# A planned attention, Fourier and MLP kernel: where the zero products begin, which engine fills buffers, how many rows are buffered, and what the planner is told of loads

## The chip, the cores and the metric

The kernel runs on one core of a Trainium2 chip. The metric is the time of one execution in device microseconds (us), the median of several runs. The profile shows one execution: TensorE (PE, with its weight loads as PEld), VectorE (DVE), ScalarE (ACT), GpSimd (POOL), the sync engine (SP) and the DMA engines.

## What is computed

Four batches of 8 heads, 768 positions and 64 elements per head. Attention is local: each chunk of 32 positions looks at 8 memory keys and a window of up to 56 keys around it. The result, laid out as 768 x 512 per batch, goes through a two-dimensional Fourier transform of which the real part is kept, and through an MLP with a residual:

```python
scores = scale * np.matmul(q_c, k_full.transpose(0, 1, 3, 2))   # per chunk of 32
a = softmax(scores); x[chunk] = np.matmul(a, v_full)
mixed = np.real(fft(fft(x, axis=1), axis=2))
u = x + mixed
un = (u - mean(u)) / sqrt(var(u) + 1e-6)
out = u + np.maximum(un @ w_ch1, 0.0) @ w_ch2                   # 512 -> 2048 -> 512
```

## The kernel before

**Work units.** Attention goes over 16 pairs of heads, n = 0 to 15, four per batch. A pair is loaded by GpSimd (`e_load_qk`, L283: q and k, cast to bf16 on the way; three buffers each) and by the sync queue (`e_load_v`, L292 to L301: v and the memory values in many short rows; four buffers `va`). TensorE turns q and k (`turn`, L310), ScalarE copies the turned q out (L319), VectorE the turned k for batch 0 and ScalarE for the rest (L337). Then come, in two halves g, the scores (`e_scores`, L348), the exponential (`e_exp`, L356, ScalarE), the product with the values (`e_values`, L369) and the normalisation (`e_norm`, L379 and L380, VectorE), which writes into `xs[b]`. The PSUM tiles `sc` and `xa` exist once each, so scores of one half wait until the exponential of the half before has read them.

**Fourier and MLP.** When a batch's `xs` is whole, the row transform runs as products with cosine and sine tables (L531 for batch 0, L437 for the others), then the column transform (L542), whose result VectorE adds into `xs` (L548). VectorE takes mean and variance (L554), ScalarE writes the centred row tile `un` in fp16 (`e_un`, L560), six tiles per batch. For batch 0 TensorE turns `un` (L567) and VectorE copies it into `unT`; for the later batches a transposing DMA on the sync queue does it (`e_flip`, L572), and the `un` buffer is free again when that DMA has landed. The MLP is `e_ch1` (`ph`, L593), ReLU on ScalarE (`hT`, L600), `e_ch2` (`pc`, L607), the residual on VectorE (L613) and the store. Its weights, eight GpSimd loads of 512 KB as written, are issued between the loads of batch 1.

**Order.** The order of all instructions on each engine is fixed when the kernel is built. Each piece of work is a task with an engine, a cost in us, a rank, the tasks it comes after, and the buffers that it takes and gives. `Plan.order` plays this through: whenever an engine is free, it gives it the task of lowest rank that is ready by the planned times. On the chip an engine then runs its instructions strictly in that order, each waiting for what it needs. The plan's numbers therefore move no instruction's duration, only its place. `LAG` is what passes between the end of a task and its use elsewhere; a load is done a lag after its bytes (`moved`, in us of wire time) have gone through its queue, plus `late` for batches after the first. TensorE's costs count double before `WARM`. The first transform and earlier pairs have lower ranks than later pairs; MLP products rank last and fill what is left.

**Zero products.** [...]So the planner puts small products with a zero matrix (`e_fill`, L650) wherever TensorE would be idle, from the moment the task `filling[0]` is placed until `filling[1]` is:

```python
if e == "PE" and self.filling and self.filling[0]["at"] is not None \
        and self.filling[1]["at"] is None:
    cost = self.FILL * (2.0 if now < self.WARM else 1.0)
```

`filling[0]` is the first zero product itself (`t_fill`, rank -1), `filling[1]` follows the first low half of batch 0's row transform.

**Fills at the start.** VectorE zeroes the last rows of the three k buffers (L634, one task) ahead of the identity cast (L628), which every turn needs; it zeroes the edges of the four v buffers (L255 to L257), computes the angles of the tables (S, then D: L668 to L676), casts and spreads the memory keys (L729, L738, L332) and copies the first k (L337). ScalarE zeroes the 32 low rows of the four v buffers (`e_low_rows`, L271): two early, two after the sines. GpSimd sets single entries of the edges to one (`e_edge_ones`). A small copy on GpSimd, the gate (L701), waits for the v of the fourth pair; q and k loads of batch 1 and the weights stand behind it.

Of the kernel before, what the change touches and what calls it, by code (L numbers as in the profile page):

```python
# [21 lines left out]
MEM0 = 32  # L22
# [14 lines left out]
class Plan:  # L37
# [1 line left out]

    LAG = {"PE": 0.2, "DMA": 1.4}
    FIRST = 45.0
    WARM = 7.0
    SLACK = 0.7
    FILL = 0.17
    filling, fill = None, None
# [14 lines left out]
    def order(self):  # L62
        now, idle, wire = 0.0, {}, {}
        waiting = {}
        for t in self.tasks:
            waiting.setdefault(t["engine"], []).append(t)
        for ts_ in waiting.values():
            ts_.sort(key=lambda t: (t["rank"], t["no"]))
        gives = []
        placed = []  # L70
        while any(waiting.values()):
            for tag in [g for g in gives if g[0] <= now]:
                gives.remove(tag)
                self.free[tag[1]] += 1
            moved = False
            for e, ts_ in waiting.items():
                if idle.get(e, 0.0) > now:
                    continue
                held = False
                for t in ts_:  # L80
                    slack = (self.SLACK if e == "PE" and now > self.FIRST and not t["filler"]
                             else 0.0)
                    if held and not t["loose"]:
                        continue
                    if any(a["done"] is None
                           or (a["end"] > now if a["engine"] == e else a["done"] > now - slack)
                           for a in t["after"]):
                        held = held or (e == "SP" and not t["loose"])
                        continue
                    if t["behind"] is not None and t["behind"]["at"] is None:  # L90
                        continue
                    need = {}
                    for tag in t["take"]:
                        need[tag] = need.get(tag, 0) + 1
                    if any(self.free[tag] < m for tag, m in need.items()):
                        held = held or (e == "SP" and not t["loose"])
                        continue
                    for tag in t["take"]:
                        self.free[tag] -= 1
                    cost = t["cost"] * (2.0 if e == "PE" and now < self.WARM else 1.0)  # L100
                    idle[e] = t["end"] = now + cost
                    if t["moved"]:
                        wire[e] = max(wire.get(e, 0.0), now + cost) + t["moved"]
                        t["done"] = t["end"] = wire[e] + self.LAG["DMA"] + t["late"]
                        if t["push"] and wire.get("SP", 0.0) > now:
                            wire["SP"] += t["moved"]
                            for o in placed:
                                if o["engine"] == "SP" and o["done"] > now:
                                    o["done"] += t["moved"]
                                    o["end"] = o["done"]  # L110
                    else:
                        t["done"] = now + cost + self.LAG.get(e, 0.07)
                    for tag in t["give"]:
                        gives.append((t["done"], tag))
                    t["at"] = now
                    placed.append(t)
                    ts_.remove(t)
                    moved = True
                    break
                else:  # L120
# [3 lines that stand above are left out]
                        idle[e] = now + cost  # L124
                        placed.append(dict(engine="PE", cost=cost, emit=self.fill, at=now,
                                           done=now + cost))
                        moved = True
            if not moved:
                times = ([v for v in idle.values() if v > now] + [g[0] for g in gives]
                         + [t["done"] + x for t in placed for x in (0.0, self.SLACK)  # L130
                            if t["done"] + x > now])
                assert times, [(t["engine"], t["no"], t["take"]) for ts_ in waiting.values()
                               for t in ts_[:2]]
                now = min(x for x in times if x > now)
        self.end = max(t["done"] for t in placed)
        return placed
# [3 lines left out]
def kernel(  # L140
# [49 lines left out]
    seq = [(b, pr) for b in range(B) for pr in (0, 2, 1, 3)]  # L190

    plan = Plan(dict(qs=NS, ks=NS, va=NV, kTb=NKT, qT=2, tr=1, sc=1, xa=1, e1=3,
                     xsb=3, fold=2, hl=1, up=4, dn=4, acc=2, mlp=2, un=3, unT=2, hT=1, osb=3))
    add = plan.add
    MLPS = 1000000

# [71 lines left out]

    def e_low_rows(i):
        low = va[i][0:MEM0].rearrange("p h t c -> p (h t c)")  # L270
        nc.scalar.copy(low, zero[0:MEM0].to_broadcast([MEM0, 2 * NT * 66]))  # L271

    def e_mkf():
        for par in range(2):
# [280 lines left out]
        nc.vector.bn_aggr(mu_of[b][:, kt, :], st6)  # L555

    def e_un(b, kt):
        un_of[b, kt] = un = fpool.tile([P, DM], FP16, tag="un", bufs=3, name="un")

        nc.scalar.activation(un, xs[b][:, kt, :], AFT.Identity, bias=mu_of[b][:, kt, 0:1],  # L560
                             scale=-1.0)
# [65 lines left out]
    def e_idb():  # L627
# [3 lines left out]
        nc.vector.tensor_copy(turn_b[:, KOFF + QP:KP], ident[0:KP, KOFF + QP:KP])  # L631

    t_idb = add("DVE", 0.5, e_idb, [t_id], rank=-16.5)
    t_kz = add("DVE", 0.8, lambda: [nc.vector.memset(ks[i][QP:KP], 0.0) for i in range(NS)],  # L634
               rank=-16.95)
    t_low, LOW = {}, 110
    for i in range(NV):
        e_ = add("DVE", 0.4, lambda i=i: e_edges(i), rank=-20 if i == 0 else -17.4 + 0.1 * i)
        t_ones[i] = add("POOL", 0.7, lambda i=i: e_edge_ones(i), [e_], rank=-3.5 if i == 0 else 2)
        t_low[i] = add("ACT", 1.45, lambda i=i: e_low_rows(i), [t_zero, e_],  # L640
                       rank=(0, 1, LOW, LOW + 1)[i])
    t_masks = add("POOL", 0.6, e_masks, rank=16)
    dz = cpool.tile([P, P], BF16)
# [33 lines left out]
            y, r, -1.0, r, ALU.mult, ALU.max), t3, rank=ANG[nm] + 3)  # L677


    kept, t_mk, t_lv, t_ck, t_after = {}, {}, {}, {}, {}  # L680
    t_norm = {}

    def last(key, n, back):
# [4 lines left out]
    def attention(n):  # L688
# [1 line left out]
        b, pr = seq[n]  # L690
        first = b == 0
        lq, lk = [add("POOL", 0.9, lambda i=i: e_load_qk(n, i), take=(("qs", "ks")[i],),
                      moved=1.3, late=0.0 if b == 0 else 2.0, behind=t_gate if n == HP else t_ck.get(n - 1),
                      rank={0: -4 + i, 1: -1.2 + 0.1 * i}.get(n)) for i in range(2)]
        lv = add("SP", 2.5, lambda: e_load_v(n), [t_ones[n] if n < NV else None],
                 take=("va",), moved=4.0, late=0.0 if b == 0 else 2.0)
        t_lv[n] = lv
        t_ck[n] = lk
        if n == HP - 1:
# [6 lines left out]
        eq = add("ACT", 0.80, lambda: e_qT(n), [tq], take=("qT",), give=("tr",),  # L706
                 rank=SINES - 0.5 if n == 0 else None)
        ktag = "acc" if first else "tr"
        tk = add("PE", 0.43, lambda: e_turn_k(n), [lk, t_idb, t_kz], take=(ktag,), give=("ks",))
        mk = t_mk[n] = add("DVE", 0.2, lambda: e_mkT(n), [t_mkT, t_kTz[n % NKT], t_mk.get(n - 1)],  # L710
                           take=("kTb",))
        ek = add(dve[0], 1.25 if dve[1] else 1.04, lambda: e_kT(n, dve[1]), [tk, mk], give=(ktag,))
        for g in range(2):
            s_ = add("PE", 0.32, lambda g=g: e_scores(n, g), [eq, ek], take=("sc",),
                     give=("qT", "kTb") if g == 1 else ())
            x_ = add("ACT", 2.4 if (n, g) == (0, 0) else 1.12, lambda g=g: e_exp(n, g),
                     [s_, t_masks, t_after.get(n)], take=("e1",), give=("sc",))
            tag = "xa"
            v_ = add("PE", 0.85, lambda g=g: e_values(n, g), [x_, lv, t_low[n % NV]], take=(tag,),
                     rank=len(plan.tasks) + (50 if (n, g) == (2, 1) else 25) if first else None,  # L720
                     give=("e1", "va") if g == 1 else ("e1",))
            take = ("xsb",) if g == 0 and n % HP == 0 else ()
            t_norm[n, g] = add("DVE", 0.78, lambda g=g: e_norm(n, g),
                               [v_, t_norm[n - n % HP, 0] if (n % HP, g) != (0, 0) else None],
                               take=take,
                               give=(tag,))
# [39 lines left out]
                    [t_angle["S"], t_angle["D"] if par == 2 else None, t_sin], rank=SINES)  # L766
    t_sines = t_sin
    for i in range(2, NV):
        t_low[i]["behind"] = t_sin
    t_neg = add("DVE", 0.6, e_negatives, [t_sines], rank=100)  # L770
    t_rows = add("DVE", 1.0, e_table_rows, [t_sines, t_neg], rank=101)
    t_idh = add("DVE", 0.25, lambda: nc.vector.tensor_copy(ident_h, ident), [t_id], rank=140)
# [15 lines left out]
    def first_fourier():  # L788
# [12 lines left out]
        for g in range(2):  # L801
            t_mid[g] = add("DVE", 0.4, lambda g=g: g_mid(g), [t_norm[2, g], t_norm[3, g]],
                           rank=len(plan.tasks) + 8)
            for par in range(2):
                for ab in range(2):
# [6 lines left out]
                    lo = add("DVE", 0.48, lambda par=par, ab=ab, g=g: g_lo(par, ab, g), [hi],  # L812
                             give=("fold",) if end else ())
                    if (par, ab, g) == (0, 0, 0):
                        plan.filling = (t_fill, add("PE", 0.0, lambda: None, [lo], give=("mlp",)))
                    tag = ("acc", "mlp")[par]
                    rw = add("PE", 2.0 if (par, ab) == (0, 1) else 1.0,
                             lambda par=par, ab=ab, g=g: g_rows(par, ab, g),
# [153 lines left out]
```

## Time and profile before

The median of three runs is 313.76 us (312.69 to 319.26); the profiled execution spans 314.6 us.

| engine | busy, us | share | instructions |
|---|---|---|---|
| PE | 298.4 | 95% | 3178 |
| PEld | 185.4 | 59% | 3178 |
| DVE | 170.4 | 54% | 371 |
| ACT | 164.8 | 52% | 293 |
| POOL | 37.5 | 12% | 76 |

| group | count | busy, us |
|---|---|---|
| first MLP product `ph` (L593) | 512 | 94.4 |
| second MLP product `pc` (L607) | 384 | 86.1 |
| values `xa` (L369) | 768 | 29.7 |
| zero products `idle` (L650) | 101 | 23.4 |
| low rows `va` on ScalarE (L271) | 4 | 5.9 |

A busy TensorE can be busy with zero products, so its share says nothing of useful work in the first slices. The chain that ended last follows the last instruction back to what released it, step by step; where it changes from PE to a DMA and back, TensorE had been waiting. In the timeline a line gives start, duration, engine, line, operation, result and operands; the bracket behind it tells how long the engine had been idle before it and what ended that. The list of DMA issues gives, for one load, the time from issue to landing.

### The profile page before, as it was taken

How to read it: one execution, taken by the hardware profiler on the slowest of the kernel's cores; microseconds unless marked ns; L12 is line 12 of the kernel's file. 1: busy time of each engine (PE TensorE's matmuls, PEld its weight loads, DVE VectorE, ACT ScalarE, POOL GpSimd, SP SyncE). 2: the span in 40 equal slices, each digit the busy share in tenths (PEclk: the TensorE clock that was granted, in tenths of full speed). 3: DMA queues.
4: the chain of work that ended last, by engine and by line, in shares of the span. 5: the costliest groups of instructions: out<-in, count | busy, mean ns of one | idle time of the engine just before them, and what ended most of it. 6: DMA issues, size and time to landing. Idle time of an engine off the chain costs nothing.

```text
span 314.6 us, 7551 instructions
## 1 busy us (share of the span) xinstructions
PE 298.4 (95%) x3178; PEld 185.4 (59%) x3178; DVE 170.4 (54%) x371; ACT 164.8 (52%) x293; POOL 37.5 (12%) x76
## 2 busy tenths in 40 slices
PE   5899999998999994999999999999999999999994
PEld 2457668876666773467577656675454454554641
DVE  7937896984398884079879488776100101002001
ACT  5657665687884372776477722753271360440710
POOL 7506322141020003000000100000200000000000
PEclk9589999999999998799999999999999999999999
DMA  6997999998991389941003301002500101101001
GB/s 113 191 167 134 209 205 197 197 198 167 180 150 44 101 134 132 134 95 42 33 35 53 52 24 44 33 2 50 150 2 33 68 2 43 57 2 67 33 35 67
DMA packets 60289, 28.93 MB, mean 92 GB/s; under 512 B 48480, under 2 KB 56672, under 8 KB 60256
## 3 DMA queue, kind: packets, MB, share of 16 engines
q1 hardware_dynamic: 47168, 11.61, 22.5%
q0 software_dynamic: 9344, 10.49, 21.1%
q10 hardware_dynamic: 3744, 6.36, 5.5%
q8 instruction: 25, 0.41, 0.6%
q14 instruction: 8, 0.07, 0.1%
HBM read 30.28 MB, written 6.29 MB: 116 GB/s over the span
## 4 chain that ended last, share of the span: by engine, by line
PE 86%; DMA 7%; SPq 2%; ACT 2%; DVE 1%; issue 1%; POOL 1%; ACTq 0%; POOLq 0%
PE pc L607 26%; PE ph L593 26%; PE xa L369 8%; PE pm L542 6%; PE idle L650 6%; PE ps L437 5%; PE ps L531 3%; PE sc L348 3%; DMA va<-in_mem_v_dram 2%; DMA qs<-in_q_dram 2%; PE trk L310 2%; PE trq L310 2%; DMA unT<-un 2%; SPq L292 2%; DVE osb L613 1%
## 5 line engine op out<-in xcount | busy, mean ns | idle before, releaser
L593 PE MATMUL ph<-unT,w_sb 128*128 128x384 f16 x512 | 94.4, 331 | 5.6 <-ACT hT L600 4.9
L600 ACT ACTIVATE hT<-ph 128x384 f16<-128x384 f32 x128 | 61.1, 492 | 66.3 <-PE ph L593 65.6
L607 PE MATMUL pc<-w_sb,hT 128*128 128x512 f16 x384 | 86.1, 380 | 0.0
L593 PEld LDWEIGHTS <-w_sb 128*128 128x128 f16 x512 | 48.6, 98 | 40.0 <-issue 11.1
L613 DVE SCALAR_TENSOR_TENSOR osb<-pc,rstd,xsb 128x512 f32<-128x512 f32 x24 | 18.0, 749 | 84.0 <-PE pc L607 84.0
L607 PEld LDWEIGHTS <-hT 128*128 128x128 f16 x384 | 36.6, 98 | 42.5 <-issue 0.3
L356 ACT ACTIVATE e<-sc,mbias 128x384 f32<-128x384 f32 x64 | 33.6, 580 | 10.7 <-PE sc L348 10.5
L369 PE MATMUL xa<-va,e 128*64 128x65 f32 x768 | 29.7, 226 | 0.8 <-DMA va<-in_mem_v_dram 0.8
L369 PEld LDWEIGHTS xa<-va,e 128*64 128x64 f32 x768 | 25.3, 138 | 7.6 <-issue 5.7
L560 ACT ACTIVATE un<-xsb,mu_s 128x512 f16<-128x512 f32 x24 | 17.1, 719 | 14.1 <-DMA unT<-un 7.8
L650 PE MATMUL idle<-dz 128*128 128x384 bf16 x101 | 23.4, 373 | 1.0 <-DVE zero L230 1.0
L449 ACT CAST up<-ps 128x386 f16<-128x386 f32 x16 | 9.7, 604 | 20.3 <-PE ps L437 14.7
L548 DVE TENSOR_TENSOR xsb<-pm,xsb 128x512 f32<-128x512 f32 x24 | 16.2, 675 | 5.7 <-PE pm L542 5.4
L380 DVE TENSOR_TENSOR xsb<-xa,zs 128x384 f32<-128x384 f32 x32 | 17.8, 557 | 1.1
L554 DVE BATCH_NORM_STATS2 st<-xsb 128x6 f32<-128x512 f32 x24 | 16.4, 682 | 0.5
L283 POOL DMA_DIRECT2D qs<-in_q_dram x16 | 10.5, 658 | 42.2 <-PE trq L310 37.0
L379 DVE RECIPROCAL zs<-xa 128x6 f32<-128x6 f32 x32 | 6.1, 189 | 17.1 <-PE xa L369 17.0
L283 POOL DMA_DIRECT2D ks<-in_k_dram x16 | 10.4, 648 | 39.1 <-PE trk L310 34.9
L319 ACT COPY qT<-trq 128x768 bf16<-128x768 bf16 x16 | 12.8, 799 | 3.7 <-PE trq L310 3.7
L650 PEld LDWEIGHTS <-dz 128*128 128x128 bf16 x101 | 9.5, 108 | 8.5 <-issue 3.0
L337 ACT COPY kTb<-trk 128x1056 bf16<-128x1056 bf16 x12 | 12.5, 1041 | 2.8 <-PE trk L310 2.8
L453 DVE TENSOR_TENSOR up<-ps,up 128x386 f16<-128x386 f32 x16 | 9.5, 597 | 8.0 <-ACT up L449 8.0
(124 smaller groups left out, 331.7 us busy)
## 6 DMA issues: line engine op xcount, KB each, us to landing
va<-in_v_dram SPq DMA_DIRECT2D x32, 220.0 KB
out_dram<-osb ACTq DMA_DIRECT2D x24, 256.0 KB
w_sb<-in_moe_w_ch_dram POOLq DMA_DIRECT2D x8, 512.0 KB, 17.0
qs<-in_q_dram POOLq DMA_DIRECT2D x16, 192.0 KB, 6.7
ks<-in_k_dram POOLq DMA_DIRECT2D x16, 192.0 KB, 6.6
va<-in_mem_v_dram SPq DMA_DIRECT2D x32, 24.0 KB
va<-in_v_dram SPq DMA_DIRECT2D x32, 22.0 KB
va<-in_v_dram SPq DMA_DIRECT2D x16, 32.0 KB
```

Source lines behind the costliest of these rows:

```text
L283: nc.gpsimd.dma_start(dst[n % NS][0:QP], src[b, 2 * pr:2 * pr + 2].rearrange("h (p j) d -> p h (j d)", j=RB))
L356: nc.scalar.activation(e1[:, :, :, ts(half, 32)], sc[:, :, 0:6, ts(half, 32)], AFT.Exp, bias=mbias[:, half:half + 1], scale=1.0 / math.sqr ...
L369: nc.tensor.matmul(xa[64 * half:64 * half + 64, st, hh, 0:65], e1[:, hh, t6, :], v1[:, hh, 6 * g + t6, 0:65], start=True, stop=True)
L380: nc.vector.tensor_tensor(xs[b][:, 3 * g:3 * g + 3, 2 * pr * D:(2 * pr + 2) * D] .rearrange("p s (h d) -> p s h d", h=2), xa[:, :, :, 0:D] ...
L542: nc.tensor.matmul(pm[:, par, :], lhs, rhs[:, par, :], start=(im == 0), stop=(im == 3))
L554: nc.vector.bn_stats(st6, xs[b][:, kt, :])
L560: nc.scalar.activation(un, xs[b][:, kt, :], AFT.Identity, bias=mu_of[b][:, kt, 0:1], scale=-1.0)
L593: nc.tensor.matmul(ph[:, 0:384], w1_sb[:, dt, ts(ht, P)], unT_of[b][:, dt, sh * 384:(sh + 1) * 384], start=(dt == 0), stop=(dt == NDT - 1))
L600: nc.scalar.activation(hT_of[b, sh][:, ht, :], ph_of.pop((b, sh, ht))[:, 0:384], AFT.Relu, bias=0.0, scale=-1.0)
L607: nc.tensor.matmul(pc_of[b, sh, stl], hT_of[b, sh][:, ht, ts(stl, P)], w2_sb[:, ht, :], start=(ht == 0), stop=(ht == NHT - 1))
L613: nc.vector.scalar_tensor_tensor(osb, pc_of.pop((b, sh, stl)), rstd_of[b][:, st:st + 1], xs[b][:, st, :], ALU.mult, ALU.add)
L650: nc.tensor.matmul(fill_of[0][:, 0:384], dz, strided(dz, 0, [[0, 3], [1, P]]), start=True, stop=True)
```

## The change

It has five parts. (1) Zero products begin when the first scores have been placed, not at the very start, and `WARM` goes from 7 to 14. (2) The planner's numbers for loads follow a trace: a GpSimd load counts as done 2.8 us after its bytes instead of 1.4, and the loads of the first four pairs have longer wire times of their own. (3) The zero rows of the first k buffer are a task of their own, ahead of the identity cast; those of the other two come after the S angles (rank -12), and the edges of v buffers 2 and 3 come among the D angles (rank -9.5, -9.4). (4) The low rows of v buffers 2 and 3 are filled by a GpSimd memset, placed behind the fourth k load, not by ScalarE. (5) `un` has six buffers instead of three. The purpose is to take waiting and filling work away from the engines that carry the start of the kernel, and to let ScalarE write all rows of a batch without waiting for a transposing DMA.

```diff
-    LAG = {"PE": 0.2, "DMA": 1.4}
+    LAG = {"PE": 0.2}
-    WARM = 7.0
+    WARM = 14.0
...
-                        t["done"] = t["end"] = wire[e] + self.LAG["DMA"] + t["late"]
+                        t["done"] = t["end"] = wire[e] + (2.8 if e == "POOL" else 1.4) + t["late"]
...
-                     xsb=3, fold=2, hl=1, up=4, dn=4, acc=2, mlp=2, un=3, unT=2, hT=1, osb=3))
+                     xsb=3, fold=2, hl=1, up=4, dn=4, acc=2, mlp=2, un=6, unT=2, hT=1, osb=3))
...
     def e_low_rows(i):
         low = va[i][0:MEM0].rearrange("p h t c -> p (h t c)")
-        nc.scalar.copy(low, zero[0:MEM0].to_broadcast([MEM0, 2 * NT * 66]))
+        if i < 2:
+            nc.scalar.copy(low, zero[0:MEM0].to_broadcast([MEM0, 2 * NT * 66]))
+        else:
+            nc.gpsimd.memset(low, 0.0)
...
-        un_of[b, kt] = un = fpool.tile([P, DM], FP16, tag="un", bufs=3, name="un")
+        un_of[b, kt] = un = fpool.tile([P, DM], FP16, tag="un", bufs=6, name="un")
...
-    t_kz = add("DVE", 0.8, lambda: [nc.vector.memset(ks[i][QP:KP], 0.0) for i in range(NS)],
-               rank=-16.95)
+    t_kz = add("DVE", 0.5, lambda: nc.vector.memset(ks[0][QP:KP], 0.0), rank=-16.95)
+    t_kzs = add("DVE", 1.0, lambda: [nc.vector.memset(ks[i][QP:KP], 0.0) for i in range(1, NS)],
+                rank=-12)
...
-        e_ = add("DVE", 0.4, lambda i=i: e_edges(i), rank=-20 if i == 0 else -17.4 + 0.1 * i)
+        e_ = add("DVE", 0.4, lambda i=i: e_edges(i), rank=(-20, -17.3, -9.5, -9.4)[i])
...
-        t_low[i] = add("ACT", 1.45, lambda i=i: e_low_rows(i), [t_zero, e_],
+        t_low[i] = add("ACT" if i < 2 else "POOL", 1.45, lambda i=i: e_low_rows(i), [t_zero, e_],
                        rank=(0, 1, LOW, LOW + 1)[i])
...
-                      moved=1.3, late=0.0 if b == 0 else 2.0, behind=t_gate if n == HP else t_ck.get(n - 1),
+                      moved=1.3 if b else (2.1, 2.1, 1.4, 1.4)[n], late=0.0 if b == 0 else 2.0,
+                      behind=t_gate if n == HP else t_ck.get(n - 1),
...
-                 take=("va",), moved=4.0, late=0.0 if b == 0 else 2.0)
+                 take=("va",), moved=4.0 if b else (4.4, 6.5, 4.9, 3.6)[n], late=0.0 if b == 0 else 2.0)
...
-        tk = add("PE", 0.43, lambda: e_turn_k(n), [lk, t_idb, t_kz], take=(ktag,), give=("ks",))
+        tk = add("PE", 0.43, lambda: e_turn_k(n), [lk, t_idb, t_kz if n == 0 else t_kzs], take=(ktag,), give=("ks",))
...
     for i in range(2, NV):
-        t_low[i]["behind"] = t_sin
+        t_low[i]["behind"] = t_ck[HP - 1]
...
-                        plan.filling = (t_fill, add("PE", 0.0, lambda: None, [lo], give=("mlp",)))
+                        plan.filling = (t_sc[0, 0], add("PE", 0.0, lambda: None, [lo], give=("mlp",)))
```

More of the change, by code (lines that the diff above doesn't have):

```diff
@@ L677 @@
             y, r, -1.0, r, ALU.mult, ALU.max), t3, rank=ANG[nm] + 3)
-    kept, t_mk, t_lv, t_ck, t_after = {}, {}, {}, {}, {}
+    kept, t_mk, t_lv, t_ck, t_after, t_sc = ({} for _ in range(6))
     t_norm = {}
@@ L715, in attention @@
                      give=("qT", "kTb") if g == 1 else ())
+            t_sc[n, g] = s_
             x_ = add("ACT", 2.4 if (n, g) == (0, 0) else 1.12, lambda g=g: e_exp(n, g),
```

## The prediction

> **What bounds the kernel now.** I read the page's slices first, then the chain of work that ended last in order of time, then the timeline around each break in it, then the times from issue to landing of single loads. Slices (40 of 7.9 us):
>
> ```profile
> PE   5899999998999994999999999999999999999994
> PEclk9589999999999998799999999999999999999999
> DMA  6997999998991389941003301002500101101001
> ```
>
> TensorE looks full from the second slice on, and the DMA engines from the second to the ninth. But in the windows, line L650, the product with zeros, fills 23.3 of the first 44.2 us. The chain shows where it stands in the way:
>
> ```profile
> 13.57 0.81 PE trk L310 x16
> 14.38 4.68 PE idle L650 x19
> 19.06 0.28 PE sc L348 x12
> ...
> 118.73 6.00 DMA unT<-un
> 124.83 0.72 ACT un L560
> 125.56 0.39 ACT hT L600
> 125.98 4.74 PE ph L593 x16
> ```
>
> Nineteen zero products lie between the last K turn and the first scores, although VectorE's copy of K, which the scores need, ends at 13.65 + 1.25 = 14.90 (first line below; the two after it are the row fills on ScalarE between exponentials):
>
> ```profile
> 13.65 1.25 DVE L337 COPY kTb<-trk 128x1056 bf16<-128x1056 bf16 x1
> 21.67 1.49 ACT L271 COPY va<-zero 32x1584 f32<-32x1584 f32 x1
> 26.54 1.50 ACT L271 COPY va<-zero 32x1584 f32<-32x1584 f32 x1
> ```
>
> Second break, 118 to 126 us: ScalarE stands at `un` until a transposing DMA has given a buffer back; behind it in its order stands the `hT` that TensorE needs:
>
> ```profile
> 124.83 0.72 ACT L560 ACTIVATE un<-xsb,mu_s 128x512 f16<-128x512 f32 x1 [5.33 <-DMA unT<-un]
> 125.98 6.12 PE L593 MATMUL ph<-unT,w_sb 128*128 128x384 f16 x24 [4.59 <-ACT hT L600]
> ```
>
> Third, what the loads allow. The GpSimd queue is backed up: q of the eighth pair, issued at 44.84, took 19.0 us (lands 63.8); its k, issued at 47.55, lands at 66.6, as TensorE comes to turn it. Soon after, values wait for a v load:
>
> ```profile
> ks<-in_k_dram POOLq DMA_DIRECT2D x1, 192.0 KB, 19.1
> ```
>
> TensorE's side of it:
>
> ```profile
> 66.65 0.55 PE L310 MATMUL trk<-turn_b,ks 100*64 100x100 bf16 x16 [0.18 <-DMA ks<-in_k_dram]
> 72.90 0.80 PE L369 MATMUL xa<-va,e 128*64 128x65 f32 x20 [0.83 <-DMA va<-in_mem_v_dram]
> ```
>
> So there are three regimes: a start-up chain to 44 us, a DMA-fed stretch to about 73, and TensorE alone after that (68.34 busy of 68.5 us from 126.5 to 195; 108.18 of 108.6 from 202 to 310.6).
>
> **What the Trainium skill says.** "TensorE: Matmul & The Clock Gate", section "What's actually happening": the array drops to half rate after an idle window of about 3.4 us and comes back after about as long busy, the window running freely. The trace agrees roughly: 2.64 us idle before 7.60 brought 0.85 us Q turns (0.53 later); from 14.31 full rate was back at 17.17, in 2.9 us; after the 4.59 us gap the clock was 0.50 in the window 125.98 to 129.80. "DMA: Bandwidth & Descriptors", section "Queues, rings and completion order": each DMA engine takes turns between queues, packet by packet; that agrees with GpSimd loads of one size taking 3.7 us (issued 26.39) when the sync queue had just run dry and 19 us later. "SBUF — State Buffer", section "Who interferes with whom": GpSimd collides with VectorE only over the shared ports, and a GpSimd instruction that only writes isn't held up by VectorE's two-input ones; no run here shows a fill this long.
>
> **Part by part.**
>
> *Zero products from the first scores on.* Gone are the fillers before the scores: all but one of the 15 at the very start (3.91 us in which TensorE has nothing to do) and the 24 of 7.6 to 19. The first scores move from 19.00 to just after the K copy. That copy ends a nearly gapless run of VectorE work, and the same work stays ahead of it in rank: ks zeros (1.57), edge fills of buffers 2 and 3 (1.3 together), the D angles (2.4); the change reorders them. So 14.90 stays and the scores start near 15.05: **-3.95**. TensorE is then cold. Scores and fillers run at half rate for about 2.9 us, to 18.0. Between first and second scores the trace has 13 fillers and two turns (3.36 us warm); the plan's 2.67 us (exponential 2.4 and lags) leaves room for about 9 beside the turns, 2.6 us warm; with 1.2 of it done by 18.0, the second scores stand at 19.4 against 22.64: **-3.2**. Bounds: -4.6 (ScalarE alone: 15.65 + 1.28 table + 1.05, then scores at 18.1) and -2.4 (all 13 fillers).
>
> *Row fills of buffers 2 and 3 to GpSimd.* 2 x 1.5 us leave ScalarE between exponentials. In the planner's costs each pushes the next exponential back about 0.85 us (1.45 less the 0.6 that ScalarE would have waited for scores): **-1.6** by the last scores of batch 0, so about **-4.8** in all there (35.71 to 30.9). On GpSimd a fill costs between 1.4 and 3.5 us: its memset of 128x384 bf16 took 424 ns, so 1584 elements 1.75 us by count and 3.5 by bytes. I take 1.75. It is placed behind the fourth k load, where GpSimd idles 13.7 us before the gate, and values need the rows only after 26 us: nothing on the path.
>
> *Zeros and edges later.* The identity cast waited for ks zeros until 7.32; without two edge fills and two zero fills ahead (1.3 + 1.05) the first Q turn waits only for its load, 6.45 instead of 7.60. The first K turn waits for its load (9.60) anyway: nothing. GpSimd's edge ones for buffer 2 now wait on an edge fill that ends near 10.6; the loads of the fourth pair queue behind them, some 1 us later. Landing then at 19.3 and 21.0, they may cost the last turns of batch 0 about 0.5 us, inside the next term.
>
> *Planned costs and lags.* They cost no instruction; they move things in the written order. Even the new costs make the planned landing of the eighth pair far earlier than the traced 63.8 and 66.6 (lag +1.4 us, gate about +3.4), so the planner still doesn't see that backlog, and I expect the same TensorE order around it.
>
> *What of -4.8 survives the loads.* The rows of the first transform, 44.3 before, could start at 39.5, and TensorE would be at the eighth Q turn at 59.7 instead of 64.48. Its load lands at 63.8. It can move only with the gate (the fourth v load, landed 25.88) and with the DMA time that lies idle: shares of 18 to 26 us and the hole at 24 to 26.3 (share 0.63), which the fifth v load can now use as its buffer comes free sooner. An upper bound is some 3.5 us, a lower one 0: the v queue runs ahead sooner and takes its turns from the q/k queue. A stall of 3 to 4 us also brings the half clock, 1.5 us or so. The 0.83 us wait for v is likely to go. I take **-1.0**, between +1 and -4.8.
>
> *Six `un` buffers.* All six rows of a batch have a buffer; no activation waits for its own batch's transposes. The 4.59 us gap goes, and with it the slow clock after it: 16 matmuls took 4.74 us, 16 at the later 1.41 per 8 take 2.82, so 1.92. Sum **-6.5**. TensorE is the bound from there to the end, so it stays. The other `un` waits (0.42, 2.06 us on ScalarE) have no gap in TensorE beside them: nothing. Bounds: -7 and, if the transposes' order on the sync queue brings a wait elsewhere, -1.
>
> Sum: 313.76 - 6.5 - 1.0 = **306.3**.
>
> **Rivals.** *A, the loads don't hold it*: the gate comes early, or MLP products are planned into the wait. Then 313.76 - 6.5 - 4.8 = 302.5. For it: the DMA's idle time at 18 to 26, and w1 landed by 47. Against: the products' inputs are turned behind the eighth Q turn in TensorE's order. *B, the wait moves*: a new in-order hole takes what six buffers give, and only the front's 1.0 is left: 312.8. For it: every order is rewritten; against: the gap has one cause, and ScalarE no other DMA to wait for. *C, slower*: stalls at the eighth pair plus cold clock (+2), a new gap like that at 121 (+6.5), the old one half gone (-3): 319.3. For it: shifting fixed orders made such gaps before; against: it needs several at once.
>
> **From these to the numbers.** Mine 0.52, A 0.20, B 0.20, C 0.08. Two per cent is 307.5. About four fifths of mine lies below it (0.42) and all of A: faster 0.62. The rest of mine, B and a quarter of C: same 0.32. Slower 0.06. The range runs from a little below A, 301.0, to nearly B, 312.0.
>
> **What would show it.** Right: first scores near 15 us with zero products only after them; no L271 on ScalarE after 7 us; no `un` waiting for a DMA, and full clock at 118 to 126, moved; a wait on q or k of the eighth pair near 60 to 66 that eats the front's gain. Wrong: the eighth k landing before 64 (A), a TensorE gap over 3 us after 100 (B or C), or first scores after 17.

## The result, and the profile after

The changed kernel takes **308.87 us** (median of four executions, 308.59 to 309.45). The kernel before, run beside it, took 312.69 to 319.93 us, median 316.51. The ratio of the two is **0.985** (95% interval 0.981 to 0.989): faster, but not by the 2% on which the forecast had put its largest chance. The ratio leaves out executions more than 1.5% above a kernel's fastest, and since 38 of 59 further executions of the kernel before (311.26 to 319.81 us) are of that kind, medians of all executions are given beside the ratios below.

The changed kernel's slices of the span (40 of 7.7 us; busy tenths of TensorE, its granted clock, busy tenths of the DMA engines):

```profile
PE   1399999999999999999989999999999999999994
...
PEclk9999999999999999999999999999999999999999
DMA  6989999999944925821361011004201101001011
```

Against the slices of before: the first two slices are emptier (1 and 3 tenths, where 5 and 8 stood; only one zero product is left there), the hole in slice 16 is gone, and the clock row has no digit below 9. The two holes are best priced by cutting both traces at one event that both have, the first product of the column transform of batch 1. Columns: stretch, its length, TensorE's busy time and matmuls, granted clock, DMA share, GB/s. Before:

```profile
0.00:109.05 109.05, 102.67 (x1542) 0.95 0.94 162
109.05:314.60 205.55, 195.75 (x1638) 0.98 0.26 55
```

After:

```profile
0.00:108.14 108.14, 96.03 (x1589) 1.00 0.99 170
108.14:307.10 198.96, 193.47 (x1566) 1.00 0.21 53
```

The front gave 0.91 us, the rest 6.59. The prediction's terms for the same stretches were -1.0 and -6.5. (The cut is not quite clean: the new order has four first and four second MLP products less ahead of it and other work more, but the busy time behind it differs by 0.3 us at most from that of a kernel with the old order and six buffers, 193.79, below.) So in this pair of traces the split came out, and yet the sum missed, 306.3 forecast against 308.87.

The break at 118 to 126 us is gone. The same window of both traces, columns: stretch, length, then busy time and instructions of PE, PEld, DVE, ACT and POOL, clock, DMA share, GB/s. Before:

```profile
118.00:126.50 8.50, 3.90 (x78) 2.58 (x77) 3.80 (x10) 2.52 (x4) 2.87 (x4) 0.81 1.16 134
```

After:

```profile
118.00:126.50 8.50, 8.50 (x128) 5.42 (x122) 5.42 (x16) 6.88 (x14) 1.61 (x2) 1.00 0.68 110
```

At the start, TensorE's timeline of the changed kernel (start, duration, engine, line, operation; in brackets how long it had stood and for what):

```profile
15.23 0.50 PE L351 MATMUL sc<-qT,kTb 64*128 64x64 bf16 x12 [2.22 <-DVE kTb L340]
...
16.70 2.10 PE L654 MATMUL idle<-dz 128*128 128x384 bf16 x6
18.73 0.88 PE L313 MATMUL trk<-turn_b,ks 100*64 100x100 bf16 x16
19.54 1.15 PE L654 MATMUL idle<-dz 128*128 128x384 bf16 x5
20.62 0.35 PE L351 MATMUL sc<-qT,kTb 64*128 64x64 bf16 x12
```

The first scores stand at 15.23 (forecast 15.05) and wait for the K copy and nothing else. But the array is cold far longer than forecast: six zero products at 16.70 take 0.35 us each, the K turn at 18.73 takes 0.88 where a later one takes 0.55, and only of the five from 19.54 (1.15 us in all) do most run at full rate. The trace's first clock record, full speed, stands at 19.91 us: half rate lasted some 4.7 us from 15.2, not 2.9.

At the eighth pair there is no wait. First what was issued at 45.99, its k load (KB as written, us from issue to landing); then TensorE's turns:

```profile
ks<-in_k_dram POOLq DMA_DIRECT2D x1, 192.0 KB, 17.8
```

```profile
64.63 0.53 PE L313 MATMUL trq<-ident_b,qs 96*64 96x96 bf16 x16
...
66.89 0.55 PE L313 MATMUL trk<-turn_b,ks 100*64 100x100 bf16 x16
```

The k load lands at 63.8, 3.1 us before its turn.

| event in the trace, us | before | after | moved | forecast |
|---|---|---|---|---|
| first scores | 19.00 | 15.23 | -3.77 | -3.95 |
| second scores | 22.64 | 20.62 | -2.02 | -3.2 |
| last scores of batch 0 | 35.71 | 32.90 | -2.81 | -4.8 |
| first row products | 44.17 | 42.40 | -1.77 | -4.8 |
| first MLP product | 67.13 | 65.10 | -2.03 | not given |
| column transform of batch 1 | 109.05 | 108.14 | -0.91 | -1.0 |

### The profile page after: what moved, and what is told of

It is laid out like the page before. It is cut to its first block, busy times and chain, and to the rows that moved or that the text cites. A ratio compares the mean times of both kernels' runs of the same rounds, so it can differ in the third digit from the quotient of the medians.

```text
span 307.1 us, 7496 instructions
## 1 busy us (share of the span) xinstructions
PE 289.5 (94%) x3148; PEld 181.5 (59%) x3148; DVE 171.2 (56%) x371; ACT 161.5 (53%) x291; POOL 40.8 (13%) x78
## 4 chain that ended last, share of the span: by engine, by line
PE 91%; DMA 2%; POOL 2%; DVE 1%; ACT 1%; issue 1%; POOLq 0%; ACTq 0%
PE ph L596 28%; PE pc L610 27%; PE xa L372 9%; PE pm L545 7%; PE ps L440 5%; PE idle L654 5%; PE ps L534 4%; PE sc L351 3%; DMA qs<-in_q_dram 2%; PE trk L313 2%; PE trq L313 2%; DVE osb L616 1%; POOL qs L286 0%; ACT hT L603 0%; PE tp L570 0%
## 5 line engine op out<-in xcount | busy, mean ns | idle before, releaser
L596 PE MATMUL ph<-unT,w_sb 128*128 128x384 f16 x512 | 91.6, 326 | 2.2 <-ACT hT L603 1.1
L596 PEld LDWEIGHTS <-w_sb 128*128 128x128 f16 x512 | 47.8, 97 | 36.8 <-issue 5.7
L654 PE MATMUL idle<-dz 128*128 128x384 bf16 x71 | 15.3, 350 | 1.0 <-DVE zero L230 1.0
L584 POOL TENSOR_SCALAR rstd<-mu_s 128x6 f32<-128x6 f32 x4 | 1.0, 245 | 102.0 <-DVE osb L616 57.7
L313 PE MATMUL trq<-ident_b,qs 96*64 96x96 bf16 x256 | 9.4, 221 | 5.1 <-DMA qs<-in_q_dram 5.1
```

Source lines behind the costliest of these rows:

```text
L313: nc.tensor.transpose(out_[64 * hh:64 * hh + 64, j * w:(j + 1) * w], src[:, hh, j * D:(j + 1) * D], eye)
L596: nc.tensor.matmul(ph[:, 0:384], w1_sb[:, dt, ts(ht, P)], unT_of[b][:, dt, sh * 384:(sh + 1) * 384], start=(dt == 0), stop=(dt == NDT - 1))
L654: nc.tensor.matmul(fill_of[0][:, 0:384], dz, strided(dz, 0, [[0, 3], [1, P]]), start=True, stop=True)
```

## The experiments

The reference trace of before stands in the table above. Each kernel's median is of all its executions; "cut" is the column transform of batch 1, "tail" what follows it.

**1. The kernel before once more.** No edit. It asks whether the gap at `un` is the same in every execution.

> The kernel before, unchanged, for a second trace. Theory T1 (the gap at the un buffers is not the same length in every execution, and the profiled one had a long one): the TensorE gap before ph near 121 us and the half-clock stretch after it differ from 4.59 us and 1.92 us of the first trace by more than 1 us, and the time is nearer to 313 than to 316. Theory T2 (the gap is fixed by the order, and the front part of the change gave something back later): the same gap within 0.3 us.

316.79 us median (312.11 to 320.31, 20 executions; ratio 1.002, 0.997 to 1.007). Its traced execution took 314.81 us. ScalarE and TensorE in its timeline:

```profile
123.30 0.72 ACT L560 ACTIVATE un<-xsb,mu_s 128x512 f16<-128x512 f32 x1 [2.79 <-DMA unT<-un]
126.16 0.72 ACT L560 ACTIVATE un<-xsb,mu_s 128x512 f16<-128x512 f32 x1 [1.38 <-DMA unT<-un]
```

```profile
124.45 2.32 PE L593 MATMUL ph<-unT,w_sb 128*128 128x384 f16 x8 [2.05 <-ACT hT L600]
127.31 3.00 PE L593 MATMUL ph<-unT,w_sb 128*128 128x384 f16 x14 [0.54 <-ACT hT L600]
```

The same instructions, in the same order, now stand 2.05 + 0.54 us where they stood 4.59. The transposes took 4.1 us from issue to the `un` that waits for them (119.19 to 123.30), against 6.1 in the first trace. The tail is 203.04 us instead of 205.55. So the gap varies in an unchanged kernel. The front does too: first scores 17.76, rows 42.32, first MLP product 65.08, all 1.2 to 2.1 us ahead of the first trace, and yet the cut at 110.06, 1 us behind it, after a wait for v of 2.31 us. What moves by 1 to 2 us between two single traces of the front is therefore no proof of anything. And the median of 20 is 3 us above the 313.76 that I had subtracted from.

**2. Six `un` buffers alone, in the kernel before.**

```diff
-    ... un=3 ...   # the planner's buffers
+    ... un=6 ...
-        ... tag="un", bufs=3 ...
+        ... tag="un", bufs=6 ...
```

> The kernel before with six un buffers instead of three, in the pool and in the planner, nothing else. T1 and T2 as I predicted the part: 6.5 us less than before in an execution like the profiled one. If the fastest executions of before have a shorter gap (T1), 3 to 5 us less than those. T3 (most of the change's gain comes from the start, six buffers alone bring under 1.5 us): 0 to 1.5 us less.

311.57 us (309.83 to 312.28, 6; ratio 0.989, 0.982 to 0.996). Against the 316.7 us of before that is -5.1. Behind the cut (windows, columns as above):

```profile
109.13:308.10 198.97, 193.79 (x1637) 1.00 0.25 57
```

Here the two halves of the `un` term can be read apart, since the order is that of before: busy time fell from 195.75 to 193.79, -1.96 (forecast 1.92 for the half clock), and TensorE's standing from 9.80 to 5.18, -4.62 (forecast 4.59 for the gap). For the traced execution the step was right to 0.1 us. Nothing came in its place; the wait for v in the front stayed:

```profile
72.96 0.80 PE L369 MATMUL xa<-va,e 128*64 128x65 f32 x20 [2.33 <-DMA va<-in_mem_v_dram]
```

**3. The changed kernel with three `un` buffers**: the two lines above the other way round.

> The changed kernel with three un buffers again. If the two parts add up, it is faster than before by what the start brings, 1.5 to 2 us (rows of the first transform 1.8 us earlier in the trace), and still has a wait of un for its own batch's transposes with a TensorE gap of 3 to 5 us near 118 to 125. If the start's gain is lost in that wait, it is as slow as before (within 0.7 us). T3 would have it within 1.5 us of the changed kernel.

314.44 us (311.91 to 315.67, 22; ratio 1.002, 0.999 to 1.006). The gap is back:

```profile
125.02 0.72 ACT L563 ACTIVATE un<-xsb,mu_s 128x512 f16<-128x512 f32 x1 [4.69 <-DMA unT<-un]
```

```profile
126.17 1.46 PE L596 MATMUL ph<-unT,w_sb 128*128 128x384 f16 x8 [3.83 <-ACT hT L603]
```

but this time the clock stayed at 1.00 after it (eight products in 1.46 us, not 2.3). This execution was the fastest of the 22; the others have a lower mean clock, 0.988 to 0.994 against its 0.997. Tail 202.6. So without the buffers the rest of the change is worth 2.3 us in medians of all executions, and by the ratio nothing. Parts by medians: -5.1 and -2.3, together -7.4; whole change 316.7 to 308.9, -7.8. By medians the parts add up; by the ratios (0.989 and 1.002, together 0.985) they do within their intervals.

**4. Only the start of the zero products, in the kernel before.**

```diff
-    WARM = 7.0
+    WARM = 14.0
...
-    plan.filling = (t_fill, add("PE", ...))
+    plan.filling = (t_sc[0, 0], add("PE", ...))
```

> The kernel before with zero products from the first scores on and WARM 14, nothing else. My prediction's step: first scores near 15.0 instead of 19.0, second scores 2 to 3.2 us earlier than 22.6. If this part alone makes the start's gain, rows of the first transform begin 1.5 to 2.5 us before 44.2 and the total is 1 to 2.5 us less; if the cold clock eats it, the rows begin within 0.7 us of 44.2 and the total is the same.

313.85 us (310.9 to 319.57, 22; ratio 0.995, 0.992 to 0.998). First scores 14.98, ahead of both traces of before (19.00 and 17.76); rows 41.82 (44.17 and 42.32); but the first MLP product at 66.65 (67.13 and 65.08) and the cut at 110.06 (109.05 and 110.06). What eats the start stands in TensorE's timeline:

```profile
64.00 0.53 PE L310 MATMUL trq<-ident_b,qs 96*64 96x96 bf16 x16 [1.81 <-DMA qs<-in_q_dram]
73.92 0.80 PE L369 MATMUL xa<-va,e 128*64 128x65 f32 x20 [1.19 <-DMA va<-in_mem_v_dram]
```

This is the wait on the eighth pair that the prediction expected of the whole change. It comes with this part alone, under the planner's old numbers for loads; and the mean clock from 60 to 80 us was 0.91.

**5. Only the planner's numbers for loads, in the kernel before** (lines abridged).

```diff
-   wire[e] + self.LAG["DMA"] + t["late"]
+   wire[e] + (2.8 if e == "POOL" else 1.4) + t["late"]
...
-   moved=1.3 / moved=4.0                  # q and k / v
+   moved=1.3 if b else (2.1, 2.1, 1.4, 1.4)[n] / moved=4.0 if b else (4.4, 6.5, 4.9, 3.6)[n]
```

> The kernel before with the planner's new numbers for loads alone (lag 2.8 us for GpSimd loads, traced wire times for the first four pairs). My prediction: no effect beyond 0.7 us. Rival, since the old numbers in the changed kernel brought back a 2.84 us wait for v and 1.7 us in all: 1 to 2 us less than before, with no v wait over 1 us at 60 to 80 us, though the first scores stay between 17 and 19.

316.08 us (314.99 to 317.7, 18; ratio 1.006, 1.003 to 1.008): no gain alone. In its trace no wait for v is left between 60 and 80 us (TensorE 19.33 busy of 20; 18.99 and 17.57 in the two traces of before), but the `un` gap is a long one:

```profile
127.33 0.72 ACT L560 ACTIVATE un<-xsb,mu_s 128x512 f16<-128x512 f32 x1 [5.41 <-DMA unT<-un]
```

The other order sends the transposes two and three at a time. Its spread is 2.7 us where that of before is 8.5.

**6. The changed kernel with the old numbers for loads**: the lines of run 5 the other way round.

> The changed kernel with the planner's old numbers for loads (1.4 us lag for all, 1.3 us for q and k, 4.0 us for v). My prediction: the numbers change no duration and hardly the order around the eighth pair, so the same total within 0.7 us. Rival: these numbers are what keeps TensorE from standing at loads of batch 1 (zero products alone had waits of 1.81 us for q and 1.19 us for v and a slow clock at 64 to 72 us); then such waits return at 60 to 75 us and the total is 1 to 2.5 us more.

310.54 us (309.44 to 312.12, 6; ratio 0.988, 0.983 to 0.993), 1.2 to 1.7 us above the two medians of the changed kernel, though the executions overlap (those go up to 310.42). The wait for v is back:

```profile
73.14 0.89 PE L372 MATMUL xa<-va,e 128*64 128x65 f32 x20 [2.84 <-DMA va<-in_mem_v_dram]
```

and the cut stands at 110.86, 2.7 us later than in the changed kernel. So numbers that cost no instruction do carry part of the front's gain in the traces.

**7. The changed kernel with all low rows on ScalarE, behind the sines, as before.** In the changed order the two fills then stand at 14.89 and 18.65, both ahead of the second scores, not between later exponentials as at 21.67 and 26.54.

```diff
-        if i < 2: nc.scalar.copy(...)
-        else:     nc.gpsimd.memset(low, 0.0)
+        nc.scalar.copy(...)
...
-        t_low[i] = add("ACT" if i < 2 else "POOL", ...
+        t_low[i] = add("ACT", ...
...
-        t_low[i]["behind"] = t_ck[HP - 1]
+        t_low[i]["behind"] = t_sin
```

> The changed kernel with the low rows of v buffers 2 and 3 on ScalarE behind the sines again, as before. My prediction's step: the last scores of batch 0 come 1.6 us later than 32.9 in the changed kernel, and the total is 0 to 1.6 us more. Rival, from the two traces: values follow values at 2.0 to 2.8 us whatever ScalarE does, since one values tile is passed back and forth between TensorE and VectorE; then the last scores move by under 0.6 us and the total by under 0.5 us.

309.1 us (307.71 to 309.76, 6; ratio 0.982, 0.977 to 0.987). Second scores 22.27 (+1.65), last scores of batch 0 34.65 (+1.75), rows +1.0, cut +1.0, median +0.2. That looks like the 1.6 us that the prediction gave the two fills, but they are not what held the second scores. ScalarE is done with them at 20.14 and then stands:

```profile
18.65 1.49 ACT L271 COPY va<-zero 32x1584 f32<-32x1584 f32 x1
22.70 1.05 ACT L356 ACTIVATE e<-sc,mbias 128x384 f32<-128x384 f32 x2 [2.55 <-PE sc L348]
```

TensorE comes late:

```profile
19.91 2.42 PE L651 MATMUL idle<-dz 128*128 128x384 bf16 x7
22.27 0.39 PE L348 MATMUL sc<-qT,kTb 64*128 64x64 bf16 x12
```

These are seven zero products at half rate, where the changed kernel has five, most of them at full rate, in 1.15 us. In this execution full rate was recorded from 22.40 us on, in the changed kernel's from 19.91. From the second to the last scores it is 12.38 us against 12.28. So the run does not measure what fills between exponentials cost, and little of the delay reaches the end.

**8. The changed kernel with the D angles and D sines later**, out of the way of the first K copy: a longer head start, to see whether the loads hold it.

```diff
-    ANG = dict(S=-18, D=-10)
+    ANG = dict(S=-18, D=90)
...
-        t_sin = add("ACT", ... 1.35, ..., [t_angle["S"], t_angle["D"] if par == 2 else None, t_sin])
+        t_sin = add("ACT", ... 2.6, ..., [..., x_last if par == 2 else None])   # x_last: last exponential of batch 0
...
-    t_rows = add("DVE", 1.0, e_table_rows, [t_sines, t_neg], rank=101)
+    t_rows = add("DVE", 1.0, e_table_rows, [t_sin, t_neg], rank=101)
```

> The changed kernel with the D angles behind the first copy of k on VectorE and the D sines behind the last exponential of batch 0 on ScalarE (two more table loads, 1.28 us each, in a stretch where ScalarE idles 3.6 us). First scores near 13 instead of 15.2. If the start still sets the end of the stretch, the rows of the first transform begin 1 to 2 us before 42.4 and the total is 0.7 to 2 us less; if loads of batch 1 now bind, waits for them appear at 60 to 75 us and the total is the same within 0.7 us.

308.66 us (307.28 to 309.33, 6; ratio 0.981, 0.976 to 0.986). First scores 13.44, second 17.65, rows 38.94: 3.5 us ahead of the changed kernel, nearly what the prediction had expected of the change itself. At the cut it is 0.9 us behind. Between stand:

```profile
53.04 0.35 PE L351 MATMUL sc<-qT,kTb 64*128 64x64 bf16 x12 [2.32 <-ACT e L359]
```

```profile
65.83 0.53 PE L313 MATMUL trq<-ident_b,qs 96*64 96x96 bf16 x16 [1.06 <-DMA qs<-in_q_dram]
```

Further waits are 0.67 us at 69.83, for an exponential, and 0.44 at 74.20, for v. Between the rows and the cut TensorE stands 4.48 us (70.09 less 65.61 busy), in the changed kernel 0.67 (65.74 less 65.07). That is 3.8 of the 4.35 us lost, the rest is busy time. The longest wait is for ScalarE, whose exponential stands behind a table load (1.28 us from 50.64); 1.5 us are waits for loads. By the medians it is 0.2 us faster than the changed kernel, which is within the spread.

**9 and 10. The changed kernel with zero products from the very start**, twice, the second time beside a repeat of the changed kernel (run 11).

```diff
-    WARM = 14.0
+    WARM = 7.0
...
-    plan.filling = (t_sc[0, 0], add("PE", ...))
+    plan.filling = (t_fill, add("PE", ...))
```

> The changed kernel with zero products from the very start and WARM 7 again. If zero products ahead of the scores are what cost the start, the first scores are back at 17.8 to 19.0, and the total is 1 to 2 us more and more spread from one execution to the next. If the loads set the end of that stretch anyway, the total is the same within 0.7 us.

> The changed kernel with zero products from the very start and WARM 7, once more beside the changed kernel. My prediction's theory (they stand in front of the first scores, -3.2 us without them): slower than the changed kernel or, once loads bind, the same. Rival from the first run of it (second scores at 20.0 instead of 20.6 though the first come 1.5 us later): the clock that they keep up is worth more than their place, and it is 1 to 2 us faster.

307.15 us (306.88 to 311.71, 6; ratio 0.977, 0.972 to 0.981) and 307.64 us (306.85 to 308.34, 6; ratio 0.979, 0.975 to 0.984).

**11. The changed kernel once more.** No edit.

> The changed kernel itself, on the chip of the three runs beside it. 308.6 to 309.5 us as before; if the zero products' place is what makes the next kernel faster, it stays 1 to 2 us behind that one here too.

309.31 us (308.58 to 310.42, 6; ratio 0.985, 0.980 to 0.990), beside run 10: 1.7 us between the medians, and the two ranges don't meet. **By the medians the variant of runs 9 and 10 is faster than both kernels**, though one of its twelve executions took 311.71 us. In the front, early zero products and late ones come out alike: cut at 107.78 and 108.80 against 108.14 and 108.42, even though the second of these four has a wait on q that the changed kernel lacks:

```profile
65.29 0.53 PE L313 MATMUL trq<-ident_b,qs 96*64 96x96 bf16 x16 [1.34 <-DMA qs<-in_q_dram]
```

The difference is in the tail, 197.80 against 198.98 us. There the changed kernel has two waits that the variant's order does not:

```profile
157.61 2.20 PE L596 MATMUL ph<-unT,w_sb 128*128 128x384 f16 x12 [0.64 <-ACT hT L603]
159.99 0.81 PE L596 MATMUL ph<-unT,w_sb 128*128 128x384 f16 x4 [0.18 <-ACT hT L603]
```

Of the 1.2 us, 0.6 are less standing (the two waits sum to 0.82), and 0.6 are less busy time (193.48 and 192.91). So the start of the zero products changed the order of work 140 us later, and that is worth more at the end than first scores 1.5 us earlier (15.23 against 16.68 and 16.79). It is the order that counts there, not the zero products as such: run 8, with late zero products, has the same short tail, 197.8. Nothing in the profile of before announced it.

**12. The same with `WARM` left at 14**, to see which of the two lines does it.

```diff
-    plan.filling = (t_sc[0, 0], add("PE", ...))
+    plan.filling = (t_fill, add("PE", ...))
```

> The changed kernel with zero products from the very start but WARM 14, so that the planner sees them at half rate until 14 us and puts fewer ahead of the first scores. If the clock matters and the place too, first scores near 15.2 and second scores before 20.0, and 0 to 1 us less than with WARM 7. If the clock is cold again at the first scores for want of enough products, second scores near 20.6 and the total as in the changed kernel.

307.32 us (306.94 to 311.39, 6; ratio 0.981, 0.975 to 0.988); four of the six lie between 306.94 and 307.57. Tail 197.8. So it is the start of the filling. The traced execution was the 311.39 one: it waits 2.31 us for q at 65.62, and its mean clock from 60 to 80 us is 0.83. The loads' stretch can still cost this family some 4 us in an execution.

## Why the prediction was right and wrong

**The step that failed is the base of the sum.** "Sum: 313.76 - 6.5 - 1.0 = 306.3" takes two terms read off one traced execution and subtracts them from the median of three others. The traced execution spans 314.6 us, longer than that median as it stands, and took 316.29 us. From its own time, 316.29 - 7.5 = 308.8; the traced execution of the changed kernel took 308.85. The base was 2.5 us short, and the miss is 2.6. Over 59 executions beside runs 1 to 4 the kernel before has a median of 316.71 us; three executions with 312.69, 313.76 and 319.26 could have warned me, as could the page itself. By the ratios the same error shows as a term that is too large: six buffers alone have 0.989, some 3.5 us of 313.76, where 6.5 were taken off.

**Behind that stands a term that has no one size.** The 6.5 us is the gap of that execution with its cold clock. By run 1 the same gap is 2.6 us in another; the tail with three buffers lasts 205.55 and 203.04 us in the kernel before, 202.6, 201.8 and 204.5 in runs 3, 4 and 5, and with six always 199.0 (the two traces of the changed kernel, runs 2, 6 and 7) or 197.8 (runs 8 to 10 and 12). Six buffers are worth 2.9 to 6.6 us; by medians 5.1. It is also why the front looks larger in medians (2.3) than in the pair of traces (0.91): against the trace of run 1 the split is 1.9 and 4.1. Two things go into what the gap costs: how long the transposes took from issue to use (3.5 to 6.1 us), and whether the clock then dropped (clock 0.50 in the first trace at 126 us; 0.61 at 124 to 128 in run 1; 1.00 in runs 3 and 4, over gaps of 3.83 and 1.66). On the second, the Trainium skill, "TensorE: Matmul & The Clock Gate", section "What's actually happening", has the array drop after an idle window of about 3.4 us and the window run freely. The clock records agree with the free window: in each trace the changes lie whole multiples of 3.41 us apart (17.38, 123.19 and 130.01 in the first), counted from a different moment in each. They don't agree with the length: in run 4 a pause of 1.81 us before the turn at 64.00 was followed by half rate from 65.79 to 69.20, while the 3.83 us of run 3 were not. Which of the two makes the 8.5 us spread of the kernel before was not taken apart by a run. The mean clock of every execution is on record, though: over the 59 its median is 0.977, and it goes with the time (correlation -0.75); in all ten executions of the changed kernel it is 0.999 or 1.000. With six buffers most sets of six executions stay within 1.5 to 2.7 us, though two have one execution 4 us out; with three and the new order (runs 3 and 5) the spread is 3.8 and 2.7, so it is not the buffers alone that make it.

**First scores** (forecast -3.95): right, -3.77, and the K copy bounds them as said.

**Second scores** (-3.2): -2.0. The mis-sized term is the cold stretch, 2.9 us forecast, 4.7 measured. The 2.9 us were misread from the warm-up in the trace of before. They were counted from the zero products at 14.31, but TensorE had been at work without a pause since 11.54:

```profile
11.54 0.85 PE L310 MATMUL trq<-ident_b,qs 96*64 96x96 bf16 x16 [0.31 <-DMA qs<-in_q_dram]
12.33 0.82 PE L650 MATMUL idle<-dz 128*128 128x384 bf16 x2
```

Its half rate ended at 17.38 by the clock record, 5.8 us after that. Where the 3.41 us steps of the clock fall differs between executions: in run 3, with the same front, full rate came at 18.36 and the second scores at 19.85, -2.8. So part of this miss is chance. The lower bound, -2.4, was too tight as well.

**Low rows off ScalarE** (-1.6 at the last scores): about -0.8 beside the second scores' gain, since the scores after them take 12.28 us (20.62 to 32.90) instead of 13.07 (the same 12.28 and 13.07 in the second traces, runs 11 and 1). No run isolates it, and run 7 does not. The fill that stood before the second exponential cost nothing at the second scores in the kernel before: TensorE came to them late for its own reasons. Nor does the pace behind that fall further in this order. In the changed kernel ScalarE waits a whole us for each of the last scores, because TensorE's written order has the values first:

```profile
30.00 0.92 PE L372 MATMUL xa<-va,e 128*64 128x65 f32 x24
30.85 0.35 PE L351 MATMUL sc<-qT,kTb 64*128 64x64 bf16 x12
31.14 0.99 PE L654 MATMUL idle<-dz 128*128 128x384 bf16 x5
32.05 0.92 PE L372 MATMUL xa<-va,e 128*64 128x65 f32 x24
32.90 0.35 PE L351 MATMUL sc<-qT,kTb 64*128 64x64 bf16 x12
```

```profile
31.31 1.05 ACT L359 ACTIVATE e<-sc,mbias 128x384 f32<-128x384 f32 x2 [1.00 <-PE sc L351]
33.35 1.05 ACT L359 ACTIVATE e<-sc,mbias 128x384 f32<-128x384 f32 x2 [1.00 <-PE sc L351]
```

Values, scores, exponential, five zero products, values: a ring of 2.05 us with one `sc` tile, in which, as I read it, a fill's time on ScalarE is only partly on the path. On GpSimd the fills cost nothing, as forecast.

**First turns** (6.45): right, 6.47. The K turn came at 10.23, not 9.60 as expected, behind a product for the memory keys that had stood 2.70 us; no effect on 15.23.

**"Planned costs and lags: nothing"**: wrong. Runs 5 and 6 show that the numbers move the order so that TensorE no longer stands for a v load (2.84 us in run 6, 0.83 to 2.33 in the old order); worth 1.2 to 1.7 us within the change.

**What survives the loads** (-1.0): right in size by luck (against the trace of run 1 it would be -1.9, by medians -2.3), and wrong in its account. The rows gained 1.8 us, not 4.8, so no wait on the eighth pair had to eat anything, and none is there: the sign that I had named for being right did not show. That a larger head start runs into the loads is shown only in part: in run 4 by 3.0 us of waits for q and v with half rate after the first, in run 8 by 1.5 us of waits out of 4.35 lost. The sign named for rival A, the eighth k landing before 64, did come (63.8: issued 1.6 us earlier and 1.3 us less on the way than before), but not A's total. Whether A's 302.5 could be had with a full 4.8 us at the rows stays open, since no run reached the rows that early without new waits on ScalarE. Rivals B and C are out: in the changed kernel no wait on TensorE behind 30 us is longer than 0.67 us.

## What to carry to other kernels

Subtract what you read in a trace from the time of the execution that was traced, and only then ask how that execution stands to the median; where runs of a kernel spread by 2%, look for a wait whose length varies, since removing it changes the spread and the mean. A start-up gain counts only as far as the next loads let it, and a planned order can shift a wait 140 us away by more than the start gained: test the edit with and without each part that is thought harmless.

## What the runs showed of the hardware that was not expected

**No clock record before the first change.** In the changed kernel the granted clock reads 1.00 in every window from 0 to 60 us, while turns take 0.84 to 0.88 us at 6.47 to 18.73 instead of 0.53 to 0.55. The trace's clock record begins only at 19.91 us, and the view counts the time before it as full. Durations are to be trusted there.

**GpSimd fills and VectorE's copies.** Two low-row fills took 2.81 us, 1.4 each, no more than the 1.5 each on ScalarE (estimate 1.75). Beside them small copies on VectorE grew. GpSimd first, VectorE next:

```profile
13.24 2.81 POOL L274 MEMSET va<- 32x1584 f32 x2
```

```profile
13.73 0.97 DVE L335 COPY kTb<-mkT 128x96 bf16<-128x96 bf16 x1
...
15.09 1.16 DVE L761 TENSOR_SCALAR odd<-cosS 128x579 f16<-128x579 f16 x1
16.17 0.29 DVE L761 TENSOR_SCALAR odd<-sinS 128x579 f16<-128x579 f16 x1
```

In run 7, where GpSimd has no fill there and VectorE's order is the same, they don't:

```profile
13.72 0.19 DVE L332 COPY kTb<-mkT 128x96 bf16<-128x96 bf16 x1
...
15.08 0.31 DVE L758 TENSOR_SCALAR odd<-cosS 128x579 f16<-128x579 f16 x1
15.30 0.30 DVE L758 TENSOR_SCALAR odd<-sinS 128x579 f16<-128x579 f16 x1
```

So the fills do it. The prediction had put them beside VectorE at no cost; the pauses agree with the Trainium skill, "SBUF — State Buffer", section "Who interferes with whom", that copies and the scalar forms in their two-port modes share a port pair with GpSimd and that the later one waits. That these instructions ran in such a mode, no view shows. The first `odd` row put back what followed on VectorE by 0.9 us (16.17 against 15.30); the K copy, and with it the first scores, came at the same time in both (K copy from 13.83 and 13.82).
